# One lock in the planner's model, lower halves on VectorE, five column blocks beside the attention

## The chip, the cores and the metric

The kernel runs on one core of a Trainium2 chip. The metric is the device time of one execution in microseconds (us). A profiled execution gives a trace of every engine: TensorE (PE, its weight loads PEld), VectorE (DVE), ScalarE (ACT), GpSimd (POOL) and SyncE (SP), which here only issues transfers.

## The reference, cut to what matters

Everything is float32. Causal attention over 2 batches, 12 heads, 448 positions, head width 64; then a gated feed-forward block with RMS norm, then a second feed-forward block:

```
attn  = softmax(mask(q @ k^T / 8)) @ v            # per head, 448 x 448
x     = attn as (896 tokens, 768)
xn    = x / sqrt(mean(x*x) + 1e-6) * rms_g
h     = silu(xn @ w_gate) * (xn @ w_val)          # 768 -> 1536
y     = h @ w_out                                 # 1536 -> 768
g     = max(0.01 * (y @ w_in), y @ w_in)          # 768 -> 2048
out   = g @ w_out2                                # 2048 -> 768
```

The weights arrive as float64 (two 32-bit words each).

## The kernel before

**Products in three passes.** Every feed-forward operand is split into an upper half, rounded to the fast float type of TensorE, and a lower half, which is the rest. A product is upper x upper, upper x lower, lower x upper: lines 568, 569 and 570, one matmul of 448 columns each.

**A weight tile** (`weight`, lines 187 to 214) is loaded as 768 columns of float64 into one of two `raw` tiles, turned into float32 in one of two `x` tiles by ACT (L202) and four DVE instructions (L203, L205, L207, L209), and split into one of four `hl` tiles: upper half on ACT (L211), lower half on POOL (L212). There are 78 such tiles. A tile waits for the reader of the tile that held its place before.

**The attention** goes through 12 pairs of heads, six per batch. `maxima` (L309, L317) finds each row's largest score, which goes to DRAM and back as a row (`md`, `mrow`); `exponents` forms the scores again (L367, L373), takes exp on ACT (L396) and cuts off the masked triangle on POOL (L403). `attend` sums the exponents (L430) and multiplies by the values (L415); the sums go to DRAM and back (`sd`, `st`), are inverted on DVE (L460, L463) and spread to all partitions through DRAM (`rd`, `rb`). POOL multiplies by the inverse (L477), ACT squares (L485), and POOL adds the square to the batch's sum (L488).

**The norm** of batch b (`norm`, lines 495 to 546) follows the batch's last pair: sum over partitions (L506), DVE (L520), the power -1/2 on POOL (L522), four diagonal tiles `dg` on DVE (L525), spread by TensorE (L513), ACT (L529), then for each of six blocks of 128 channels: scale on DVE (L534), upper half on ACT (L537), lower half on POOL (L544), in the second batch on DVE for every other block (L540).

**Beside the attention of batch 1** the gate and value products of batch 0 run for the first EARLY = 6 column blocks of w_gate and w_val, in banks 4 and 5 alone, 36 matmuls a block. Each ends in `gate_out` (lines 603 to 620): silu on ACT (L611), product on DVE (L613), upper half on ACT (L616), lower half (L618) on POOL for the early blocks and on DVE for the others. The weights of the last two early blocks stay in `hl` for batch 1; those of the first EARLY - 2 are loaded and prepared a second time at the end of this stage ("again"). The other products follow when the attention is done, 2448 matmuls of lines 568 to 570 in all.

**The order of the work** is fixed in advance by the class `Order` (lines 19 to 92). Every step has an engine, an estimated cost, its dependences, a rank, a delay `late` after its end (the transfers) and an earliest time `at`. `emit` takes the engine that can start first, on it the ready step with the lowest rank, and moves a model clock; the instructions are then issued in the order of the model's starts. Each engine executes its own list in that order, so a step that is late in fact holds up what is listed behind it. All transfers are issued by SP, from one list. A lower rank goes first: pair i has ranks from 10i - 30 to 10i + 27, the norm of batch 1 has 88 and less, the early blocks 99 and up, their weights 87 and up.

Of the kernel before, what the change touches and what calls it, by code (L numbers as in the profile page):

```python
# [13 lines left out]
ALU = mybir.AluOpType  # L14
# [4 lines left out]
class Order:  # L19

    SWITCH = 0.09
    HOP = 0.12
# [5 lines left out]

    def add(self, eng, cost, fn, r=(), w=(), rank=0.0, late=0.0, mode=None, at=0.0):
        n = len(self.steps)
        deps = set()
        for k in r:
            deps.update(self.written.get(k, ()))
        for k in w:
            deps.update(self.written.get(k, ()))
            deps.update(self.read.get(k, ()))
        for k in w:  # L40
            self.written[k] = [n]
            self.read[k] = []
        for k in r:
            if k not in w:
                self.read.setdefault(k, []).append(n)
        self.steps.append((eng, cost, fn, deps, rank, late, mode, at))
        return n

    def emit(self):
        steps = self.steps  # L50
        left = [len(s[3]) for s in steps]
        users = [[] for _ in steps]
        for n, s in enumerate(steps):
            for d in s[3]:
                users[d].append(n)
        est = [s[7] for s in steps]
        ready = {}
        for n, s in enumerate(steps):
            if not left[n]:
                ready.setdefault(s[0], []).append(n)  # L60
        free = {}
        mode = {}
        start = [0.0] * len(steps)
        for _ in steps:
            best = None
            for eng, ns in ready.items():
                if ns:
                    t = max(free.get(eng, 0.0), min(est[n] for n in ns))
# [4 lines left out]
            n = min(  # L73
                (n for n in ready[eng] if est[n] <= t),
                key=lambda n: (steps[n][4] + (6 if steps[n][6] != cur else 0), n),
            )
            ready[eng].remove(n)
            _, cost, _, _, _, late, m, _ = steps[n]
            if m != cur:
                cost += self.SWITCH  # L80
                mode[eng] = m
            start[n] = t
            free[eng] = t + cost
            done = t + cost + late
            for u in users[n]:
                est[u] = max(est[u], done + (0.0 if steps[u][0] == eng and not late else self.HOP))
                left[u] -= 1
                if not left[u]:
                    ready.setdefault(steps[u][0], []).append(u)
        for n in sorted(range(len(steps)), key=lambda n: (start[n], n)):  # L90
            steps[n][2]()
        return max(free.values())
# [3 lines left out]
def causal_attention_two_ffns(  # L96
# [53 lines left out]
    def f32(ap):  # L150
        return ap.bitcast(F32)
# [5 lines left out]

    EARLY = 6
    NBIG = B * KF2
# [27 lines left out]
    def weight(key, rank, at=0.0):  # L187
# [14 lines left out]
        add("ACT", 0.85, lambda: nc.scalar.activation(x[:, :w], tf, AF.Abs), r=[kr], w=[kx], rank=rank)  # L202
        add("DVE", 0.62, lambda: nc.vector.tensor_scalar(  # L203
            x[:, :w], x[:, :w], LEAST, MOST, ALU.max, ALU.min), r=[kx], w=[kx], rank=rank)
        add("DVE", 0.6, lambda: nc.vector.tensor_scalar(  # L205
            xb, xb, 3, 0x3FFFFFF8, ALU.logical_shift_left, ALU.bitwise_and), r=[kx], w=[kx], rank=rank)
        add("DVE", 1.0, lambda: nc.vector.scalar_tensor_tensor(  # L207
            xb, top, 0xC0000000, xb, ALU.bitwise_and, ALU.bitwise_or), r=[kr, kx], w=[kx], rank=rank)
        add("DVE", 1.0, lambda: nc.vector.scalar_tensor_tensor(  # L209
            xb, low, 29, xb, ALU.logical_shift_right, ALU.bitwise_or), r=[kr, kx], w=[kx], rank=rank)  # L210
# [145 lines left out]
    def exponents(i):  # L356
# [23 lines left out]
        for kbs in groups:  # L380
# [12 lines left out]
            for j in range(2):  # L393
# [8 lines left out]
                d = d[:, :, lead:lead + P]  # L402
                add("POOL", 0.45, lambda d=d: nc.gpsimd.affine_select(  # L403
                    out=d, in_=d, compare_op=ALU.is_ge, fill=0.0, base=0, pattern=[[0, 2], [1, P]],
                    channel_multiplier=-1), w=[("p", i % 2, j, kb) for kb in kbs], rank=10 * i - 6)

    def attend(i):
# [16 lines left out]
        def sums():  # L424
            for kb in range(KB):
                for j in range(2):
# [7 lines left out]
                    )  # L434

        pk = [("p", i % 2, j, kb) for j in range(2) for kb in range(KB)]
        add("PE", 1.95 if last else 0.95, sums, r=pk, w=["sm"], rank=10 * i + 5, mode=128)
# [11 lines left out]
        else:  # L449
# [5 lines left out]
            for j in range(2):  # L455
# [3 lines left out]
            st = sts[i % NB]  # L459
            add("DVE", 0.15, lambda: nc.vector.scalar_tensor_tensor(  # L460
                out=rs[i % NB], in0=st[:, 0], scalar=1e-9, in1=st[:, 1], op0=ALU.add, op1=ALU.add),
# [12 lines left out]
        if i + 1 < NPAIR:  # L474
            add("ACT", 0.57, lambda: nc.scalar.copy(x, AV[:, :S]), r=["av"], w=[("x32", i % NX32)],
                rank=10 * i + 5)
            add("POOL", 1.1, lambda: nc.gpsimd.tensor_tensor(out=x, in0=x, in1=rbs[i % NB], op=ALU.mult),  # L477
                r=[("rb", i % NB, 0), ("rb", i % NB, 1)], w=[("x32", i % NX32)], rank=10 * i + 26)
        else:
            add("DVE", 0.65, lambda: nc.vector.tensor_tensor(  # L480
                out=x, in0=AV[:, :S], in1=rbs[i % NB], op=ALU.mult),
                r=["av", ("rb", i % NB, 0), ("rb", i % NB, 1)], w=[("x32", i % NX32)], rank=10 * i + 26)
        a = acc[:, b * S:(b + 1) * S]
        sq = sqs[i % 2] if hp else a
        add("ACT", 0.57, lambda: nc.scalar.activation(sq, x, AF.Square), r=[("x32", i % NX32)],  # L485
            w=[("sq", i % 2) if hp else ("acc", b)], rank=10 * i + 27)
        if hp:
            add("POOL", 1.1, lambda: nc.gpsimd.tensor_tensor(out=a, in0=a, in1=sq, op=ALU.add),  # L488
                r=[("sq", i % 2)], w=[("acc", b)], rank=10 * i + 27)

# [4 lines left out]
    def norm(b):  # L495
# [15 lines left out]
        def spread():  # L511
# [9 lines left out]
            r=[k0], w=[("ms", b)], rank=rank - 30)  # L521
        add("POOL", 1.4, lambda: nc.gpsimd.tensor_tensor(out=rt, in0=ms, in1=nhalf, op=ALU.pow),  # L522
            r=[("ms", b)], w=[("rt", b)], rank=rank - 30)
        for c in range(NC):
            add("DVE", 0.25, lambda c=c: nc.vector.tensor_scalar(  # L525
                dgs[c], ident[:C, :C], rt[:, c:c + 1], None, ALU.mult),
                r=[("rt", b)], w=[("dg", c)], rank=rank - 30)
        add("PE", 0.95, spread, r=[("dg", c) for c in range(NC)], w=[k1], rank=rank - 20, mode=128)
        add("ACT", 0.57, lambda: nc.scalar.copy(rsb, B1[:, :S]), r=[k1], w=["rs"], rank=rank - 20)  # L529
        for i in range(KD):  # L530
            n = (b * NP + i) % NX32
            x = x32[n]
            hi, lo = (xn[:, e, i, b * S:(b + 1) * S] for e in range(2))
            add("DVE", 0.75, lambda x=x, i=i: nc.vector.scalar_tensor_tensor(  # L534
                out=x, in0=x, scalar=gsb[:, i:i + 1], in1=rsb, op0=ALU.mult, op1=ALU.mult),
                r=["rs"], w=[("x32", n)], rank=rank + i)
            add("ACT", 0.57, lambda x=x, hi=hi: nc.scalar.copy(hi, x),  # L537
                r=[("x32", n)], w=[("xh", b, i)], rank=rank + i)
            if b and i % 2:
                add("DVE", 0.7, lambda x=x, hi=hi, lo=lo: nc.vector.tensor_tensor(  # L540
                    out=lo, in0=x, in1=f32(hi), op=ALU.subtract),
                    r=[("x32", n), ("xh", b, i)], w=[("xn", b, i)], rank=rank + i)
            else:
                add("POOL", 1.1, lambda x=x, hi=hi, lo=lo: nc.gpsimd.tensor_tensor(  # L544
                    out=lo, in0=x, in1=f32(hi), op=ALU.subtract),
                    r=[("x32", n), ("xh", b, i)], w=[("xn", b, i)], rank=rank + i)

# [55 lines left out]
    def gate_out(fc, b, rank, room, lower):  # L603
# [4 lines left out]
        def view(e):  # L608
# [8 lines left out]
            r=[("sg", s)] + room, w=[("big", n)], rank=rank)  # L617
        add(*lower, lambda: (nc.gpsimd if lower[0] == "POOL" else nc.vector).tensor_tensor(  # L618
            out=view(1), in0=sgs[s], in1=f32(view(0)), op=ALU.subtract),
# [27 lines left out]
    for n in range(NPAIR + AHEAD):  # L647
# [32 lines left out]
    for again in (False, True):  # L680
        for fc in range(EARLY - 2) if again else range(EARLY - 2, KF):
# [5 lines left out]
            for b in range(1 if kept or again else 0, B):  # L687
                for nm in "gv":
                    gate(nm, fc, b, rank, again=again)
                gate_out(fc, b, rank, ["room"], ("DVE", 0.7))  # L690

# [22 lines left out]
    for fc in range(KF2):  # L714
        rank = FF + 60 + fc
        weight(("i", fc), rank - 1)
        for b in range(B):
# [8 lines left out]
            def view(e, g=g):  # L726
# [8 lines left out]
                r=[("sg", s), "room"], w=[("big", g)], rank=rank)  # L735
            add("DVE", 0.7, lambda s=s, view=view: nc.vector.tensor_tensor(  # L736
                out=view(1), in0=sgs[s], in1=f32(view(0)), op=ALU.subtract),
# [65 lines left out]
```

## Time and profile before

| | |
|---|---|
| median of 3 runs | 648.8 us (648.07, 648.8, 654.26) |
| profiled execution | 649.93 us |
| its span, first to last instruction | 648.1 us |
| instructions | 8720 |
| TensorE busy in matmuls | 616.4 us (95%) |
| VectorE busy | 445.8 us (69%) |
| ScalarE busy | 265.3 us (41%) |
| GpSimd busy | 229.6 us (35%) |
| moved by DMA | 74.56 MB, mean 115 GB/s |

"Busy" is the share of the span in which the engine has an instruction in work. TensorE's matmuls overlap, so its busy share counts a slow or half-filled stretch as full; the granted clock and the number of matmuls in a stretch say more. An instruction of DVE or POOL that stands still because the other engine holds something also counts as busy.

### The profile page before, as it was taken

How to read it: one execution, taken by the hardware profiler on the slowest of the kernel's cores; microseconds unless marked ns; L12 is line 12 of the kernel's file. 1: busy time of each engine (PE TensorE's matmuls, PEld its weight loads, DVE VectorE, ACT ScalarE, POOL GpSimd, SP SyncE). 2: the span in 40 equal slices, each digit the busy share in tenths (PEclk: the TensorE clock that was granted, in tenths of full speed). 3: DMA queues.
4: the chain of work that ended last, by engine and by line, in shares of the span. 5: the costliest groups of instructions: out<-in, count | busy, mean ns of one | idle time of the engine just before them, and what ended most of it. 6: DMA issues, size and time to landing. Idle time of an engine off the chain costs nothing.

```text
span 648.1 us, 8720 instructions
## 1 busy us (share of the span) xinstructions
PE 616.4 (95%) x3280; PEld 531.4 (82%) x3280; DVE 445.8 (69%) x694; ACT 265.3 (41%) x406; POOL 229.6 (35%) x176
## 2 busy tenths in 40 slices
PE   8987878979889999999999999999999999999997
PEld 5654446657779999999889999999999999999996
DVE  6465579768878696558988974599999883444300
ACT  3446655664333433334433423355554543223210
POOL 1224556965542332233333322232233223132300
PEclk7799987998889999999999999999999999999999
DMA  5254642332323144322444443233223323344100
GB/s 179 76 156 130 205 135 80 114 115 90 120 97 106 67 141 141 131 98 98 146 147 147 146 147 102 93 127 116 98 99 101 123 85 119 137 139 131 62 28 30
DMA packets 21331, 74.56 MB, mean 115 GB/s; under 512 B 5220, under 2 KB 8232, under 8 KB 21288
## 3 DMA queue, kind: packets, MB, share of 16 engines
q1 hardware_dynamic: 21288, 73.99, 34.2%
q8 instruction: 26, 0.43, 0.3%
q14 instruction: 17, 0.14, 0.1%
HBM read 71.07 MB, written 2.91 MB: 114 GB/s over the span
## 4 chain that ended last, share of the span: by engine, by line
PE 76%; DVE 14%; DMA 4%; issue 3%; ACT 1%; POOL 1%; SPq 1%; DVEq 0%; ACTq 0%; POOLq 0%
PE bank L568 22%; PE bank L569 22%; PE bank L570 22%; DVE x L207 3%; PE bank L415 2%; PE bank L373 2%; DMA md<-mt 2%; DVE x L203 2%; DVE x L534 2%; DVE x L209 2%; DVE x L205 1%; PE bank L309 1%; DMA st<-sd 1%; PE bank L367 1%; DVE bank L317 1%
## 5 line engine op out<-in xcount | busy, mean ns | idle before, releaser
L212 POOL TENSOR_TENSOR hl<-x,hl 128x768 fp32r<-128x768 f32 (+1 forms) x78 | 155.1, 1990 | 315.1 <-ACT hl L211 300.6
L568 PE MATMUL bank<-xn,hl 128*128 128x448 f32 x480 | 178.8, 372 | 2.7 <-DVE sg L613 2.7
L569 PE MATMUL bank<-xn,hl 128*128 128x448 f32 x480 | 177.0, 369 | 0.0
L570 PE MATMUL bank<-xn,hl 128*128 128x448 f32 x480 | 176.9, 368 | 0.0
L569 PE MATMUL bank<-big,hl 128*128 128x448 f32 x336 | 122.9, 366 | 1.2 <-DVE big L618 1.2
L570 PE MATMUL bank<-big,hl 128*128 128x448 f32 x336 | 122.9, 366 | 0.7 <-POOL hl L212 0.7
L568 PE MATMUL bank<-big,hl 128*128 128x448 f32 x336 | 122.8, 365 | 0.0
L202 ACT ACTIVATE x<-raw 128x768 f32<-128x768 f32 (+1 forms) x78 | 69.1, 887 | 111.8 <-POOL hl L212 77.2
L203 DVE TENSOR_SCALAR x<-x 128x768 f32<-128x768 f32 (+1 forms) x78 | 51.2, 656 | 81.5 <-ACT x L202 81.5
L207 DVE SCALAR_TENSOR_TENSOR x<-raw,x 128x768 uint32<-128x768 uint32 (+1 forms) x78 | 100.4, 1287 | 2.5
L568 PEld LDWEIGHTS bank<-xn,hl 128*128 128x128 f32 x480 | 91.3, 190 | 12.7 <-ACT xn L537 3.3
L569 PEld LDWEIGHTS bank<-xn,hl 128*128 128x128 f32 x480 | 91.4, 191 | 7.3
L570 PEld LDWEIGHTS bank<-xn,hl 128*128 128x128 f32 x480 | 91.3, 190 | 7.4
L211 ACT CAST hl<-x 128x768 fp32r<-128x768 f32 (+1 forms) x78 | 63.7, 816 | 65.0 <-PE bank L569 37.8
L209 DVE SCALAR_TENSOR_TENSOR x<-raw,x 128x768 uint32<-128x768 uint32 (+1 forms) x78 | 79.6, 1021 | 1.4
L569 PEld LDWEIGHTS bank<-big,hl 128*128 128x128 f32 x336 | 63.1, 188 | 6.5 <-DVE big L618 1.5
L570 PEld LDWEIGHTS bank<-big,hl 128*128 128x128 f32 x336 | 63.1, 188 | 6.1 <-POOL hl L212 1.1
L568 PEld LDWEIGHTS bank<-big,hl 128*128 128x128 f32 x336 | 63.1, 188 | 5.0
L317 DVE CUSTOM_DVE_ANT_0 bank<-bank,maskw 112x224 f32<-112x224 f32 (+2 forms) x96 | 41.8, 464 | 25.1 <-PE bank L309 23.9
L205 DVE TENSOR_SCALAR x<-x 128x768 uint32<-128x768 uint32 (+1 forms) x78 | 49.4, 633 | 1.8
L736 DVE TENSOR_TENSOR big<-sg,big 128x448 fp32r<-128x448 f32 x32 | 45.6, 1424 | 0.0
L403 POOL TENSOR_SCALAR_AFFINE_SELECT p<-p 128x256 f32<-128x256 f32 x48 | 23.6, 503 | 48.9 <-ACT p L396 47.9
(69 smaller groups left out, 526.9 us busy)
## 6 DMA issues: line engine op xcount, KB each, us to landing
raw<-in_out SPq DMA_DIRECT2D x24, 768.0 KB
raw<-in_gate SPq DMA_DIRECT2D x16, 768.0 KB
raw<-in_val SPq DMA_DIRECT2D x16, 768.0 KB
raw<-in_in SPq DMA_DIRECT2D x16, 768.0 KB
qk<-in_qk SPq DMA_DIRECT2D x12, 448.0 KB
v<-in_v SPq DMA_DIRECT2D x12, 256.0 KB
raw<-in_out SPq DMA_DIRECT2D x6, 512.0 KB
out<-sg SPq DMA_DIRECT2D x12, 224.0 KB
```

Source lines behind the costliest of these rows:

```text
L202: add("ACT", 0.85, lambda: nc.scalar.activation(x[:, :w], tf, AF.Abs), r=[kr], w=[kx], rank=rank)
L203: add("DVE", 0.62, lambda: nc.vector.tensor_scalar(x[:, :w], x[:, :w], LEAST, MOST, ALU.max, ALU.min), r=[kx], w=[kx], rank=rank)
L205: add("DVE", 0.6, lambda: nc.vector.tensor_scalar(xb, xb, 3, 0x3FFFFFF8, ALU.logical_shift_left, ALU.bitwise_and), r=[kx], w=[kx], rank=rank)
L207: add("DVE", 1.0, lambda: nc.vector.scalar_tensor_tensor(xb, top, 0xC0000000, xb, ALU.bitwise_and, ALU.bitwise_or), r=[kr, kx], w=[kx], ra ...
L209: add("DVE", 1.0, lambda: nc.vector.scalar_tensor_tensor(xb, low, 29, xb, ALU.logical_shift_right, ALU.bitwise_or), r=[kr, kx], w=[kx], ra ...
L211: add("ACT", 0.85, lambda: nc.scalar.copy(hl[:, 0, :w], x[:, :w]), r=[kx], w=[kh], rank=rank)
L212: add("POOL", 1.95, lambda: nc.gpsimd.tensor_tensor(out=hl[:, 1, :w], in0=x[:, :w], in1=f32(hl[:, 0, :w]), op=ALU.subtract), r=[kx, kh], w ...
L317: nc.vector.tensor_tensor_reduce(out=s, in0=s, in1=maskw[:, S - w:S], scale=-1.0, scalar=3.0e38, op0=ALU.add, op1=ALU.min, accum_out=m[:, ...
L568: nc.tensor.matmul(o, hi, xh, start=s, stop=False, skip_group_check=True)
L569: nc.tensor.matmul(o, hi, xl, start=False, stop=False, skip_group_check=True)
L570: nc.tensor.matmul(o, lo, xh, start=False, stop=e, skip_group_check=True)
L736: add("DVE", 0.7, lambda s=s, view=view: nc.vector.tensor_tensor(out=view(1), in0=sgs[s], in1=f32(view(0)), op=ALU.subtract), r=[("sg", s) ...
```

## The change

The change does these things; costs in the model are in us.

- A step may be marked `port=True`. Such steps, on DVE and POOL, follow one another in the model, whichever of the two they are on.
- The lower half of a weight goes from POOL (L212) to DVE, in the norm all lower halves go to DVE, and so do those of the early blocks.
- The four diagonals of a norm go from DVE to ACT.
- EARLY is 5 instead of 6; the rank of the early blocks is 40 higher, so behind every step of the attention, and their weights may load from 30 us on instead of 40.
- The steps after the inverse (L477, L480, L485, L488) get the rank 10i + 10 instead of 10i + 26 or 27, and 10i - 20 in the last pair of each batch.

```diff
+    def add(..., port=False):
...
+        def begin(n):
+            return max(est[n], port_free) if steps[n][8] else est[n]
...
+                    t = max(free.get(eng, 0.0), min(begin(n) for n in ns))
...
+            if port:
+                port_free = t + cost
...
-    EARLY = 6
+    EARLY = 5
...
-        add("POOL", 1.95, lambda: nc.gpsimd.tensor_tensor(
+        add("DVE", 0.95, port=True, fn=lambda: nc.vector.tensor_tensor(
             out=hl[:, 1, :w], in0=x[:, :w], in1=f32(hl[:, 0, :w]), op=ALU.subtract),
...
+        own = 10 * i + (10 if (i + 1) % NP else -20)
...
-            add("DVE", 0.25, lambda c=c: nc.vector.tensor_scalar(
-                dgs[c], ident[:C, :C], rt[:, c:c + 1], None, ALU.mult),
+            add("ACT", 0.3, lambda c=c: nc.scalar.activation(
+                dgs[c], ident[:C, :C], AF.Copy, scale=rt[:, c:c + 1]),
...
-            if b and i % 2:
-                add("DVE", 0.7, lambda x=x, hi=hi, lo=lo: nc.vector.tensor_tensor(
...
-                add("POOL", 1.1, lambda x=x, hi=hi, lo=lo: nc.gpsimd.tensor_tensor(
+            add("DVE", 0.65, port=True, fn=lambda x=x, hi=hi, lo=lo: nc.vector.tensor_tensor(
...
-        return 10.0 * (NP + 3 + fc) + 9
+        return 10.0 * (NP + 7 + fc) + 9
...
-            weight((nm, fc, False), early_rank(fc) - 12, at=40.0 + 8 * (2 * fc + n))
+            weight((nm, fc, False), early_rank(fc) - 12, at=30.0 + 8 * (2 * fc + n))
...
-                    gate_out(fc, 0, early_rank(fc) - 10, [], ("POOL", 1.15))
+                    gate_out(fc, 0, early_rank(fc) - 10, [], ("DVE", 0.65, True))
```

Marked with the port are the DVE steps of a weight (L203, L205, L207, L209, L212), L403, L460, L477, L488, L522, L534, the lower halves of the norm, and L618 and L736.

## Rows read from the trace of the kernel before

**Rows 1.** The page: busy tenths of PE and granted clock in 40 slices.

```profile
PE   8987878979889999999999999999999999999997
PEclk7799987998889999999999999999999999999999
```

**Rows 2.** Windows of each stage: length, busy us (x instructions) by engine, clock, DMA.

```profile
0.00:100.00 100.00, 84.92 (x626) 52.70 (x626) 61.60 (x224) 49.72 (x81) 36.36 (x64) 0.88 0.46 144
100.00:184.40 84.40, 73.32 (x407) 55.15 (x405) 70.24 (x97) 45.30 (x70) 57.98 (x45) 0.90 0.29 98
184.40:320.00 135.60, 135.60 (x663) 125.61 (x664) 101.19 (x117) 51.85 (x77) 42.38 (x23) 0.99 0.34 117
320.00:330.00 10.00, 8.15 (x39) 6.81 (x38) 9.02 (x10) 3.99 (x6) 3.67 (x2) 1.00 0.47 159
330.00:640.00 310.00, 310.00 (x1532) 287.35 (x1531) 203.75 (x249) 113.35 (x173) 89.25 (x44) 1.00 0.33 110
```

**Rows 3.** Windows of 20 us between 100 and 200 us, same columns.

```profile
100.00:120.00 20.00, 16.59 (x110) 11.01 (x108) 19.61 (x39) 9.55 (x17) 16.28 (x15) 0.83 0.23 70
...
140.00:160.00 20.00, 16.63 (x84) 11.49 (x83) 12.79 (x19) 11.66 (x17) 11.63 (x11) 0.83 0.27 91
160.00:180.00 20.00, 18.35 (x89) 16.25 (x88) 18.17 (x22) 8.38 (x14) 12.54 (x9) 0.91 0.34 119
180.00:200.00 20.00, 17.35 (x80) 15.64 (x79) 14.72 (x18) 7.26 (x12) 8.45 (x5) 0.91 0.22 79
```

**Rows 4.** PE's waits, 100 to 185 us: for whom, us in total, times, longest.

```profile
PE bank L513 <- DVE dg L525: 3.6, 2, 2.0
PE bank L367 <- ACT p L396: 3.4, 1, 3.4
PE bank L568 <- DVE sg L613: 2.7, 1, 2.7
```

**Rows 5.** DVE by line, 100 to 184 us: busy us, mean ns | idle before.

```profile
L207 DVE SCALAR_TENSOR_TENSOR x<-raw,x 128x768 uint32<-128x768 uint32 x9 | 13.4, 1492 | 0.3
L534 DVE SCALAR_TENSOR_TENSOR x<-x,gsb,rsb 128x448 f32<-128x448 f32 x12 | 11.0, 974 | 0.2 <-ACT rsb L529 0.2
L209 DVE SCALAR_TENSOR_TENSOR x<-raw,x 128x768 uint32<-128x768 uint32 x9 | 10.6, 1175 | 0.2
L203 DVE TENSOR_SCALAR x<-x 128x768 f32<-128x768 f32 x9 | 8.8, 974 | 5.7 <-ACT x L202 5.7
L205 DVE TENSOR_SCALAR x<-x 128x768 uint32<-128x768 uint32 x9 | 7.0, 776 | 0.2
...
L525 DVE TENSOR_SCALAR dg<-ident,rt 112x112 f32<-112x112 f32 x8 | 5.7, 770 | 0.0
...
L540 DVE TENSOR_TENSOR xn<-x,xn 128x448 fp32r<-128x448 f32 x2 | 2.2, 1089 | 0.0
```

**Rows 6.** Single lines over the whole span: duration ns, min/median/max, first and last start.

```profile
L203 DVE TENSOR_SCALAR x<-x x78: 427/560/1574, 54.0 to 610.0; 128x768 f32<-128x768 f32 x72, 128x512 f32<-128x512 f32 x6
L209 DVE SCALAR_TENSOR_TENSOR x<-raw,x x78: 683/953/2485, 62.2 to 611.7; 128x768 uint32<-128x768 uint32 x72, 128x512 uint32<-128x512 uint32 x6
L534 DVE SCALAR_TENSOR_TENSOR x<-x,gsb,rsb x12: 672/680/1583, 107.8 to 182.5; 128x448 f32<-128x448 f32 x12
L525 DVE TENSOR_SCALAR dg<-ident,rt x8: 265/268/2550, 101.9 to 172.5; 112x112 f32<-112x112 f32 x8
L618 DVE TENSOR_TENSOR big<-sg,big x18: 610/616/2219, 199.3 to 328.1; 128x448 fp32r<-128x448 f32 x18
L212 POOL TENSOR_TENSOR hl<-x,hl x78: 1283/1851/2582, 75.5 to 619.5; 128x768 fp32r<-128x768 f32 x72, 128x512 fp32r<-128x512 f32 x6
```

**Rows 7.** PE's waits, 20 to 100 us, as in Rows 4.

```profile
PE bank L367 <- DMA mrow<-md: 5.9, 2, 3.4
PE bank L415 <- POOL p L403: 2.9, 2, 2.1
```

**Rows 8.** ACT lines: table load and a small copy, count, busy us, mean ns.

```profile
L611 ACT ACT_TABLE_LOAD x3 | 3.8, 1283 | 0.1
...
L529 ACT COPY rsb<-bank 128x448 f32<-128x448 f32 x2 | 1.1, 529 | 3.2 <-PE bank L513 3.2
```

More of the change, by code (lines that the diff above doesn't have):

```diff
@@ L30, in __init__, with add @@
         self.read = {}
-    def add(self, eng, cost, fn, r=(), w=(), rank=0.0, late=0.0, mode=None, at=0.0):
+    def add(self, eng, cost, fn, r=(), w=(), rank=0.0, late=0.0, mode=None, at=0.0, port=False):
         n = len(self.steps)
@@ L45, in add @@
                 self.read.setdefault(k, []).append(n)
-        self.steps.append((eng, cost, fn, deps, rank, late, mode, at))
+        self.steps.append((eng, cost, fn, deps, rank, late, mode, at, port))
         return n
@@ L61, in emit @@
         free = {}
+        port_free = 0.0
         mode = {}
         start = [0.0] * len(steps)
+        def begin(n):
+            return max(est[n], port_free) if steps[n][8] else est[n]
         for _ in steps:
@@ L67, in emit @@
                 if ns:
-                    t = max(free.get(eng, 0.0), min(est[n] for n in ns))
+                    t = max(free.get(eng, 0.0), min(begin(n) for n in ns))
                     if best is None or t < best[0]:
@@ L73, in emit @@
             n = min(
-                (n for n in ready[eng] if est[n] <= t),
+                (n for n in ready[eng] if begin(n) <= t),
                 key=lambda n: (steps[n][4] + (6 if steps[n][6] != cur else 0), n),
@@ L77, in emit @@
             ready[eng].remove(n)
-            _, cost, _, _, _, late, m, _ = steps[n]
+            _, cost, _, _, _, late, m, _, port = steps[n]
+            if port:
+                port_free = t + cost
             if m != cur:
@@ L402, in exponents @@
                 d = d[:, :, lead:lead + P]
-                add("POOL", 0.45, lambda d=d: nc.gpsimd.affine_select(
+                add("POOL", 0.45, port=True, fn=lambda d=d: nc.gpsimd.affine_select(
                     out=d, in_=d, compare_op=ALU.is_ge, fill=0.0, base=0, pattern=[[0, 2], [1, P]],
@@ L459, in attend @@
             st = sts[i % NB]
-            add("DVE", 0.15, lambda: nc.vector.scalar_tensor_tensor(
+            add("DVE", 0.15, port=True, fn=lambda: nc.vector.scalar_tensor_tensor(
                 out=rs[i % NB], in0=st[:, 0], scalar=1e-9, in1=st[:, 1], op0=ALU.add, op1=ALU.add),
@@ L476, in attend @@
                 rank=10 * i + 5)
-            add("POOL", 1.1, lambda: nc.gpsimd.tensor_tensor(out=x, in0=x, in1=rbs[i % NB], op=ALU.mult),
-                r=[("rb", i % NB, 0), ("rb", i % NB, 1)], w=[("x32", i % NX32)], rank=10 * i + 26)
+            add("POOL", 1.1, port=True, fn=lambda: nc.gpsimd.tensor_tensor(out=x, in0=x, in1=rbs[i % NB], op=ALU.mult),
+                r=[("rb", i % NB, 0), ("rb", i % NB, 1)], w=[("x32", i % NX32)], rank=own)
         else:
@@ L481, in attend @@
                 out=x, in0=AV[:, :S], in1=rbs[i % NB], op=ALU.mult),
-                r=["av", ("rb", i % NB, 0), ("rb", i % NB, 1)], w=[("x32", i % NX32)], rank=10 * i + 26)
+                r=["av", ("rb", i % NB, 0), ("rb", i % NB, 1)], w=[("x32", i % NX32)], rank=own)
         a = acc[:, b * S:(b + 1) * S]
@@ L485, in attend @@
         add("ACT", 0.57, lambda: nc.scalar.activation(sq, x, AF.Square), r=[("x32", i % NX32)],
-            w=[("sq", i % 2) if hp else ("acc", b)], rank=10 * i + 27)
+            w=[("sq", i % 2) if hp else ("acc", b)], rank=own)
         if hp:
-            add("POOL", 1.1, lambda: nc.gpsimd.tensor_tensor(out=a, in0=a, in1=sq, op=ALU.add),
-                r=[("sq", i % 2)], w=[("acc", b)], rank=10 * i + 27)
+            add("POOL", 1.1, port=True, fn=lambda: nc.gpsimd.tensor_tensor(out=a, in0=a, in1=sq, op=ALU.add),
+                r=[("sq", i % 2)], w=[("acc", b)], rank=own)
     dgs = ring(NC, [C, C], F32, "dg")
@@ L521, in norm @@
             r=[k0], w=[("ms", b)], rank=rank - 30)
-        add("POOL", 1.4, lambda: nc.gpsimd.tensor_tensor(out=rt, in0=ms, in1=nhalf, op=ALU.pow),
+        add("POOL", 1.4, port=True, fn=lambda: nc.gpsimd.tensor_tensor(out=rt, in0=ms, in1=nhalf, op=ALU.pow),
             r=[("ms", b)], w=[("rt", b)], rank=rank - 30)
         for c in range(NC):
-            add("DVE", 0.25, lambda c=c: nc.vector.tensor_scalar(
-                dgs[c], ident[:C, :C], rt[:, c:c + 1], None, ALU.mult),
+            add("ACT", 0.3, lambda c=c: nc.scalar.activation(
+                dgs[c], ident[:C, :C], AF.Copy, scale=rt[:, c:c + 1]),
                 r=[("rt", b)], w=[("dg", c)], rank=rank - 30)
@@ L533, in norm @@
             hi, lo = (xn[:, e, i, b * S:(b + 1) * S] for e in range(2))
-            add("DVE", 0.75, lambda x=x, i=i: nc.vector.scalar_tensor_tensor(
+            add("DVE", 0.75, port=True, fn=lambda x=x, i=i: nc.vector.scalar_tensor_tensor(
                 out=x, in0=x, scalar=gsb[:, i:i + 1], in1=rsb, op0=ALU.mult, op1=ALU.mult),
@@ L538, in norm @@
                 r=[("x32", n)], w=[("xh", b, i)], rank=rank + i)
-            if b and i % 2:
-                add("DVE", 0.7, lambda x=x, hi=hi, lo=lo: nc.vector.tensor_tensor(
-                    out=lo, in0=x, in1=f32(hi), op=ALU.subtract),
-                    r=[("x32", n), ("xh", b, i)], w=[("xn", b, i)], rank=rank + i)
-            else:
-                add("POOL", 1.1, lambda x=x, hi=hi, lo=lo: nc.gpsimd.tensor_tensor(
-                    out=lo, in0=x, in1=f32(hi), op=ALU.subtract),
-                    r=[("x32", n), ("xh", b, i)], w=[("xn", b, i)], rank=rank + i)
+            add("DVE", 0.65, port=True, fn=lambda x=x, hi=hi, lo=lo: nc.vector.tensor_tensor(
+                out=lo, in0=x, in1=f32(hi), op=ALU.subtract),
+                r=[("x32", n), ("xh", b, i)], w=[("xn", b, i)], rank=rank + i)
     turn = [0]
@@ L617, in gate_out @@
             r=[("sg", s)] + room, w=[("big", n)], rank=rank)
-        add(*lower, lambda: (nc.gpsimd if lower[0] == "POOL" else nc.vector).tensor_tensor(
+        add(*lower[:2], port=lower[2], fn=lambda: (nc.gpsimd if lower[0] == "POOL" else nc.vector).tensor_tensor(
             out=view(1), in0=sgs[s], in1=f32(view(0)), op=ALU.subtract),
@@ L689, in causal_attention_two_ffns @@
                     gate(nm, fc, b, rank, again=again)
-                gate_out(fc, b, rank, ["room"], ("DVE", 0.7))
+                gate_out(fc, b, rank, ["room"], ("DVE", 0.65, True))
     for dc in range(KD):
@@ L735, in causal_attention_two_ffns @@
                 r=[("sg", s), "room"], w=[("big", g)], rank=rank)
-            add("DVE", 0.7, lambda s=s, view=view: nc.vector.tensor_tensor(
+            add("DVE", 0.65, port=True, fn=lambda s=s, view=view: nc.vector.tensor_tensor(
                 out=view(1), in0=sgs[s], in1=f32(view(0)), op=ALU.subtract),
```

8 lines of the change are left out of this document (4 added, 4 removed).

## The prediction

> **What bounds the kernel now.** I read the slices first, then the windows, then what PE waits for in the windows that fall short. The slices show two regimes: PE at 7 to 9 tenths and a granted clock of 7 to 9 up to about 190 us, then both full to the end, but for one slice [rows 1]. The windows say the same in numbers [rows 2]. From 330 to 640 us PE issues 1532 instructions in 310 us without a gap, 0.202 us each, at clock 1.00; 184 to 320 us has no gap either. No work of another engine can shorten these stretches. Before 184.4 us PE lacks 15.1 us in the first 100 and 11.1 us in the next 84.4, at mean clocks of 0.88 and 0.90; 1.85 us are missing between 320 and 330. The matmuls are the same after the change, since a smaller EARLY only moves 36 of them, 7.3 us, out of the attention stage into the full stretch. So the time can change only by what PE loses before 190 us, and around 325.
>
> The stretch that the change touches is 100 to 184.4 us. PE's waits there are few and have names [rows 4]: 3.6 us on the norm's diagonals (L525), 3.4 us on an exponent (L396), 2.7 us on the product that frees a gate bank (L613), 9.7 us together. They come with clock: the windows in which they lie are granted 0.83, 0.83, 0.91 and 0.91 of full speed [rows 3], which at 20 us each is up to 0.17 + 0.17 + 0.09 + 0.09 = 0.52 windows, 10.4 us, lost beside the waits (the mean between the two levels, 1.2 and 2.4 GHz). That is 20.1 us at most.
>
> Behind the waits stands DVE, busy 70.2 of 84.4 us [rows 2], but not with work. Its lines take much longer there than their medians over the whole span [rows 5, 6]: L207 1.49 us (it has two SBUF inputs and the size of L209, 0.95), L534 0.97 against 0.68, L209 1.18 against 0.95, L203 0.97 against 0.56, L205 0.78 (like L203, 0.56), L525 0.77 against 0.27, L540 1.09 against 0.62 (L618's form). With the counts: 4.9 + 3.5 + 2.0 + 3.7 + 2.0 + 4.0 + 0.9 = 21.0 us of standing still, while POOL is busy 58.0 us, above all with L212 at 1.85 us.
>
> **The change part by part.**
>
> *Lower halves to DVE.* On DVE the trace has no L212. Below it lies L618, the same subtraction on 448 columns, 0.62 us, above it the POOL form, 1.85; I take L209, also 768 columns and two SBUF inputs: 0.95 [rows 6]. In 100 to 184 us this adds nine times 0.95 for weights, nine times 0.62 in the norms and five times 0.62 in the early blocks: 8.6 + 5.6 + 3.1 = 17.3 us. It takes away the 21.0 us of standing still as far as POOL's long steps caused it; L403, L477, L488 and L522 remain.
>
> *Diagonals to ACT.* DVE loses 8 x 0.27 = 2.1 us. On ACT no such tile is in the trace; between nothing and the 0.53 of a 448-column copy [rows 8] I take 0.3, nearer the 0.27 that it took on DVE. Four are 1.2 us on the norm's path, where two waits of 3.6 us now stand.
>
> *EARLY 5.* Two weights fewer, 2 x (0.56 + 0.56 + 0.95 + 0.95) = 6.0 us of DVE, and one L613, 0.6. The two are also not prepared a second time later. DVE in this stretch: 70.2 + 17.3 - 21.0 - 2.1 - 6.6 = 58 us, for PE work that is 7.3 us shorter. DVE is no longer what the stage waits for.
>
> *Ranks.* Early blocks and weights now stand behind every pair, and the squares of pairs 5 and 11 go first. So both norms start earlier and pair 11 no longer competes with weights. On POOL the listed order gains too: no 1.85 us step stands ahead of L403 or L488. I give this no gain of its own; it is how the 9.7 us go. What is late next: in a row that is filled by rank, a step that waits on a transfer holds what is listed behind it, L403 behind L477 on POOL, every DVE step behind L460. Such waits exist: 5.9 us in two on `mrow` and 2.9 us in two on L403 before 100 us [rows 7].
>
> *Weights from 30 us.* Four loads, of 768 KB each, reach SP's list and the DMA earlier, beside the small round trips of the pairs. It may move the 5.9 us, double them, or empty them; I take zero, with 5.9 to both sides.
>
> *Silu among exponents.* A change between L611 and L396 loads a table, 1.28 us; three are at L611 and two at L396 [rows 8]. With the gates in the gaps of the pairs there may be one change each way for five blocks, five more, 6.4 us of ACT. ACT is busy 45.3 of 84.4 us; on PE's path lies only a load before an exponent. I take none, and up to 6.4.
>
> The Trainium skill ("ScalarE: Activation LUTs", "Table sets: the hidden batching unit") advises to do all calls of one set before the other, which speaks against these ranks; it puts a switch at about 2.7 us with its drain. The trace agrees on the load, 1.283 us, and shows the exponent right behind it, so I keep 1.28; by the page five more switches would be 13.3 us (an estimate).
>
> *The full stretch.* Each of its weights costs DVE 0.95 more, hidden under PE: a block of w_in needs 3.97 + 2 x 1.24 = 6.5 us of DVE for 36 x 0.202 = 7.3 us of PE. The cover fails where weights are prepared again for one batch: 2 x 3.97 + 1.24 = 9.2 us against 7.3. Three such columns fall behind by 5.7 us, against four columns before that lost 1.85. Four `hl` tiles, two columns or 14.6 us, are the lead. I take no change; bounds: 1.85 less, and 5.7 - 1.85 = 3.9 more.
>
> **The sum.** Removed: 20.1 us at most. I give back half, 9.7: two new waits of the size of those on `mrow`, 2.95 us each [rows 7], and 1.9 us of clock with each (0.09 of a window of 20). The span goes from 648.1 to 637.7, the execution (1.83 longer) from 649.9 to 639.5. The median shown, 648.8, stands 1.1 below that execution, so 638.4; with half a us for one more table load, **639**.
>
> **Rivals.** *A: the wait changes its name.* Exponents stand behind silus and tables on ACT (6.4 us), L403 behind L477, and PE waits as often as now: of the 10.4 gained 6.4 and a window's clock, 1.9, go, and the time is 647. For it: the 3.4 us on L396, the longest wait, already was one on ACT. Against it: ACT is half idle.
>
> *B: slower; the stage keeps its end.* If pair 11 and its norm are paced by the DRAM round trips and not by DVE, xn of batch 1 is ready when it was, and the early blocks that filled the time until then are 36 matmuls short: PE stands for 7.3 us, and the time is 656. It decides at one point: the first product on batch 1's xn must start 7.3 us earlier than now to break even. For it: the waits before 100 us are on transfers [rows 7]. Against it: none of the three after 100 is [rows 4].
>
> *C: all of it goes.* No new waits: 648.8 - 20 = 629.
>
> *D: POOL was not the cause,* DVE's long instructions stay long. Then the 17.3 us come on top of 70.2 - 8.7, DVE is full for the stage, and nothing is gained: 648 to 652. Against it: the 21 us vanish in the medians, so they are not the instructions' own.
>
> **How the numbers follow.** Forecast 0.54, A 0.20, B 0.14, C 0.07, D 0.05. One per cent, about what a measurement of this kernel tells from no change, is 642.3 and 655.3 us. The forecast's own range, with 5.9 for the early loads, is 633 to 645; some 0.47 of its 0.54 is below 642.3, with C 0.54 faster. B is over 655.3 in about 0.12 of its 0.14, with a little of D 0.13 slower; 0.33 within. The range from 630 to 654 leaves out most of C and B.
>
> **What would show it.** L207, L209 and L534 at 0.96, 0.95 and 0.68 us in the attention stage; no POOL step over 1.2 us but the power; no PE wait on `dg` and under 1 us on L613; the 1033 PE instructions that stand before 184.4 us now done by about 174; the full stretch unchanged at 0.202 us. It is wrong if PE's gaps before that point are as many as now under other names (A), if batch 1's first product comes no earlier (B), or if gaps open around the weights prepared again or in the blocks of w_in.

## The result and the profile after

The changed kernel takes 623.4 us (median; 622.2 to 624.6), the kernel before 648.4 beside it: a ratio of 0.960, interval 0.955 to 0.966. That is 25 us, where 10 were forecast, and below the range. Some executions of a kernel run in a slower state: medians, ratios and intervals from here on are of the others, but the traces of `b_port`, `a_oldrank`, `a_own`, `a_at34`, `a_late` and `a_hop11` are of such slower executions.

The profiled execution has a span of 621.1 us against 648.1. The windows of its stages come first, in the columns of [rows 2]; in the lines of the changed kernel L573 to L575 are the three passes (568 to 570 before), L375 to L381 the scores, L220 the weights' lower half, L549 the norm's.

```profile
0.00:100.00 100.00, 87.53 (x670) 56.77 (x672) 69.25 (x241) 55.85 (x94) 36.55 (x64) 0.90 0.49 153
100.00:184.40 84.40, 83.28 (x476) 68.71 (x476) 72.75 (x117) 46.23 (x75) 18.72 (x19) 1.00 0.33 107
184.40:320.00 135.60, 135.60 (x671) 125.69 (x670) 101.44 (x143) 53.76 (x76) 0.00 (x0) 1.00 0.37 127
320.00:330.00 10.00, 10.00 (x51) 9.28 (x50) 8.27 (x12) 4.21 (x6) 0.00 (x0) 1.00 0.49 159
330.00:610.00 280.00, 280.00 (x1384) 259.52 (x1383) 180.72 (x260) 104.53 (x157) 0.00 (x0) 1.00 0.32 104
```

From 330 us on PE issues 1384 instructions in 280 us, 0.202 us each, as before. Everything was won ahead of that. From 100 to 184.4 us PE now stands still for 1.1 us instead of 11.1, and its clock is 1.00 throughout instead of 0.90, worth at most 0.10 x 84.4 = 8.4. In the first 100 us it stands still for 12.5 instead of 15.1, at 0.90 instead of 0.88, 2.6 + 2.0. The 1.85 us near 325 are gone, and 184 to 320 has its full clock, 1.4. Together 10.0 + 8.4 + 4.6 + 1.85 + 1.4 = 26.3 of the 27.0 us, an account in which each share of the clock is an upper bound, since a low clock costs nothing while PE stands still.

What PE waits for after 100 us, the counterpart of [rows 4], are two small items (up to 200 us; none comes later):

```profile
PE bank L574 <- DVE xn L549: 0.7, 1, 0.7
PE bank L573 <- ACT xn L547: 0.4, 1, 0.4
```

DVE's lines from 100 to 184 us, in the form of [rows 5] (L215 was L207, L544 was L534, L217 was L209, L213 was L205, L211 was L203):

```profile
L215 DVE SCALAR_TENSOR_TENSOR x<-raw,x 128x768 uint32<-128x768 uint32 x11 | 10.8, 985 | 0.1
L217 DVE SCALAR_TENSOR_TENSOR x<-raw,x 128x768 uint32<-128x768 uint32 x11 | 10.4, 946 | 0.2
L220 DVE TENSOR_TENSOR hl<-x,hl 128x768 fp32r<-128x768 f32 x10 | 9.5, 953 | 4.4 <-ACT hl L219 4.4
L549 DVE TENSOR_TENSOR xn<-x,xn 128x448 fp32r<-128x448 f32 x12 | 7.8, 684 | 0.3 <-ACT xn L547 0.2
L544 DVE SCALAR_TENSOR_TENSOR x<-x,gsb,rsb 128x448 f32<-128x448 f32 x10 | 7.3, 768 | 0.5 <-ACT rsb L539 0.5
L213 DVE TENSOR_SCALAR x<-x 128x768 uint32<-128x768 uint32 x11 | 7.1, 641 | 0.3
L211 DVE TENSOR_SCALAR x<-x 128x768 f32<-128x768 f32 x11 | 6.0, 548 | 1.5 <-ACT x L210 1.5
```

The standing still is all but gone: 0.99 us for 1.49, 0.95 for 1.18, 0.77 for 0.97, 0.64 for 0.78, 0.55 for 0.97. The weights' subtraction takes 0.95 us on DVE, the 0.95 that was estimated, against 1.85 on POOL. DVE is as busy in this stretch as before (72.8 us against 70.2; 58 were forecast), but it has eleven weights in it instead of nine.

### The profile page after: what moved, and what is told of

Same layout as the page of the kernel before. It is cut to its first block, busy times and chain, and to the rows that moved or that the text cites. A ratio compares the mean times of both kernels' runs of the same rounds, so it can differ in the third digit from the quotient of the medians.

```text
span 621.1 us, 8620 instructions
## 1 busy us (share of the span) xinstructions
PE 604.0 (97%) x3280; PEld 526.7 (85%) x3280; DVE 432.4 (70%) x769; ACT 265.6 (43%) x408; POOL 55.3 (9%) x83
## 4 chain that ended last, share of the span: by engine, by line
PE 91%; DMA 4%; DVE 3%; issue 1%; ACT 0%; SPq 0%; POOL 0%; ACTq 0%
PE bank L573 27%; PE bank L574 26%; PE bank L575 26%; PE bank L381 3%; PE bank L423 3%; PE bank L375 2%; PE bank L317 2%; PE bank L438 1%; DMA md<-mt 1%; DMA mrow<-md 1%; DVE bank L325 1%; DMA raw<-in_gate 1%; PE bank L633 1%; DMA rd<-r 1%; DVE x L544 1%
## 5 line engine op out<-in xcount | busy, mean ns | idle before, releaser
L573 PE MATMUL bank<-xn,hl 128*128 128x448 f32 x480 | 176.6, 368 | 0.4 <-ACT xn L547 0.4
L574 PE MATMUL bank<-xn,hl 128*128 128x448 f32 x480 | 175.5, 366 | 0.7 <-DVE xn L549 0.7
L575 PE MATMUL bank<-xn,hl 128*128 128x448 f32 x480 | 175.3, 365 | 0.0
L575 PE MATMUL bank<-big,hl 128*128 128x448 f32 x336 | 122.7, 365 | 0.0
L573 PE MATMUL bank<-big,hl 128*128 128x448 f32 x336 | 122.7, 365 | 0.0
L220 DVE TENSOR_TENSOR hl<-x,hl 128x768 fp32r<-128x768 f32 (+1 forms) x76 | 72.1, 948 | 60.5 <-ACT hl L219 58.6
L573 PEld LDWEIGHTS bank<-xn,hl 128*128 128x128 f32 x480 | 90.2, 188 | 9.7 <-issue 1.7
L574 PEld LDWEIGHTS bank<-xn,hl 128*128 128x128 f32 x480 | 90.2, 188 | 8.2 <-DVE xn L549 1.1
L575 PEld LDWEIGHTS bank<-xn,hl 128*128 128x128 f32 x480 | 90.2, 188 | 7.1
L219 ACT CAST hl<-x 128x768 fp32r<-128x768 f32 (+1 forms) x76 | 61.9, 815 | 72.0 <-PE bank L574 53.8
L210 ACT ACTIVATE x<-raw 128x768 f32<-128x768 f32 (+1 forms) x76 | 67.5, 888 | 57.8 <-DVE hl L220 37.6
L217 DVE SCALAR_TENSOR_TENSOR x<-raw,x 128x768 uint32<-128x768 uint32 (+1 forms) x76 | 72.2, 950 | 1.4
L215 DVE SCALAR_TENSOR_TENSOR x<-raw,x 128x768 uint32<-128x768 uint32 (+1 forms) x76 | 71.8, 945 | 1.4
L575 PEld LDWEIGHTS bank<-big,hl 128*128 128x128 f32 x336 | 63.1, 188 | 5.0
L573 PEld LDWEIGHTS bank<-big,hl 128*128 128x128 f32 x336 | 63.1, 188 | 5.0
L211 DVE TENSOR_SCALAR x<-x 128x768 f32<-128x768 f32 (+1 forms) x76 | 41.7, 549 | 33.2 <-ACT x L210 33.0
L213 DVE TENSOR_SCALAR x<-x 128x768 uint32<-128x768 uint32 (+1 forms) x76 | 42.5, 559 | 2.0
L404 ACT ACTIVATE p<-bank 128x512 f32<-128x512 f32 x48 | 26.3, 594 | 22.1 <-PE bank L381 22.0
L381 PE MATMUL bank<-qk 64*128 64x448 f32 (+3 forms) x192 | 34.1, 431 | 0.0
```

The costliest lines, as they stand in the source:

```text
L211: add("DVE", 0.62, port=True, fn=lambda: nc.vector.tensor_scalar(x[:, :w], x[:, :w], LEAST, MOST, ALU.max, ALU.min), r=[kx], w=[kx], rank= ...
L213: add("DVE", 0.6, port=True, fn=lambda: nc.vector.tensor_scalar(xb, xb, 3, 0x3FFFFFF8, ALU.logical_shift_left, ALU.bitwise_and), r=[kx], w ...
L215: add("DVE", 1.0, port=True, fn=lambda: nc.vector.scalar_tensor_tensor(xb, top, 0xC0000000, xb, ALU.bitwise_and, ALU.bitwise_or), r=[kr, k ...
L217: add("DVE", 1.0, port=True, fn=lambda: nc.vector.scalar_tensor_tensor(xb, low, 29, xb, ALU.logical_shift_right, ALU.bitwise_or), r=[kr, k ...
L220: add("DVE", 0.95, port=True, fn=lambda: nc.vector.tensor_tensor(out=hl[:, 1, :w], in0=x[:, :w], in1=f32(hl[:, 0, :w]), op=ALU.subtract), ...
L381: nc.tensor.matmul(bank[:, off:off + w], keys, t[r, 1, kb * P:], start=False, stop=True, skip_group_check=True,)
```

## The experiments

All ratios are against the kernel before, run on the same chip. Three theories stood first: **L**, POOL's long steps held DVE; **R**, the ranks put the attention first; **M**, the planner knows the lock.

**One part alone, on the kernel before.** `b_low`: the lower halves to DVE.

```diff
-        add("POOL", 1.95, lambda: nc.gpsimd.tensor_tensor(
+        add("DVE", 0.95, lambda: nc.vector.tensor_tensor(
             out=hl[:, 1, :w], ...
-            if b and i % 2:
+            if True:
...
-                    gate_out(fc, 0, early_rank(fc) - 10, [], ("POOL", 1.15))
+                    gate_out(fc, 0, early_rank(fc) - 10, [], ("DVE", 0.65))
```

Expected: 

> The kernel before, with only the lower halves (weights, norm, early blocks) moved from POOL to DVE; ranks, six early blocks, diagonals on DVE and the planner's costs without a lock stay. Theory L (POOL's long steps held DVE): DVE's long instructions shrink to their medians, and most of the 25 us come from this alone, 648 to about 630. Theory R (the ranks that put the attention first): this alone brings 5 us or less, 643 to 648, since pair 11 and its norm still stand behind weights and gates. Theory M (the planner's knowledge of the lock): 645 or more, since the order is still planned without it.

Measured: 634.1 us, 0.977 (0.968 to 0.985). Over half of the gain, some 15 us (10 to 21 by the interval), and the only part that brings much by itself. L207, L209 and L534 take 1.04, 1.10 and 0.75 us in the stage, near their medians.

`b_rank`: the ranks (`own` is 10 * i + 10, and 10 * i - 20 in pairs 5 and 11) and the load time.

```diff
-        return 10.0 * (NP + 3 + fc) + 9
+        return 10.0 * (NP + 7 + fc) + 9
-            weight(..., at=40.0 + 8 * (2 * fc + n))
+            weight(..., at=30.0 + 8 * (2 * fc + n))
-                ... rank=10 * i + 26)
+                ... rank=own)
```

Expected: 

> The kernel before, with only the ranks changed: early blocks and their weights behind every pair, weights from 30 us on, squares of pairs 5 and 11 first. Lower halves stay on POOL. Theory R: most of the 25 us, about 630, pair 11's last product (L480 before at 159.5 us) comes some 20 us earlier. Theory L: DVE still stands still behind POOL, 643 or more. Theory M: 645 or more.

Measured: 651.6 us, 1.006 (1.001 to 1.011): nothing won. The last pair did come earlier, its last inverse on DVE at 142.3 us instead of 155.6. But the fill that is left then is held up by the diagonals on DVE and by the lower halves on POOL. PE's longest waits in this kernel from 100 to 200 us:

```profile
PE bank L514 <- DVE dg L526: 3.9, 1, 3.9
PE bank L571 <- POOL hl L212: 3.5, 4, 1.2
PE bank L570 <- POOL xn L545: 2.4, 1, 2.4
PE bank L507 <- POOL acc L489: 1.7, 1, 1.7
```

`b_early5` (`EARLY = 5` alone) and `b_port` (the lock in the plan alone).

Expected: 

> The kernel before, with five early blocks instead of six and nothing else. All theories: no gain of its own, since the number of matmuls is the same; 648 if the stage ends earlier by the 7.3 us of the block, up to 656 if the stage keeps its end (the slower rival of the prediction).

Measured: 643.3 us, 0.989 (0.982 to 0.996). One block less is a small gain, not the 7.3 us of loss of the slower rival.

Expected: 

> The kernel before, with only the planner's lock between DVE and POOL (all work stays on its engine; the steps that the change marks are marked, and three lower halves on DVE cost 0.65 instead of 0.7 in the plan). Theory M: the order is now planned with the lock, most of the 25 us, about 630. Theories L and R: the lock is still there on the chip and the attention is not first, 645 to 650.

Measured: 661.1 us, 1.020 (1.013 to 1.026). Planned with the lock while the long steps stay on POOL, the kernel is slower. M alone falls.

**One part taken back, from the changed kernel.** `a_noport` takes out the two lines that move `port_free`; `a_poolall` puts L220, the norm's blocks and the early blocks' lower halves back on POOL as in the kernel before (three of the norm's stay on DVE), with their lock; `a_oldrank` restores all three rank settings; `a_early6` sets EARLY to 6.

Expected: 

> The changed kernel, planned without the lock (the marks have no effect); everything else stays. If the lock in the plan matters once the long steps have left POOL: 628 or more. If only the place of the lower halves matters: 623 as the changed kernel, since what is left on POOL (L403, L477, L488) is short.

Measured: 632.4 us, 0.973 (0.966 to 0.979), the first case.

Expected: 

> The changed kernel with the lower halves back on POOL (weights, norm blocks and early blocks as before), the lock in the plan, the ranks and five blocks kept. Theory L: the gain is gone, 645 to 660, and DVE's long instructions are back at 1.2 us and more. Theory R: 630 or less.

Measured: 645.3 us, 0.996 (0.992 to 1.001). With the lower halves on POOL again nothing of the gain is left, and DVE's L215 and L217 take 1.19 and 1.31 us in the stage, as theory L has it.

Expected: 

> The changed kernel with the old ranks (early blocks and weights among the pairs, weights from 40 us, squares at 10i + 26). Ranks alone brought nothing while the lower halves were on POOL. If they still bring nothing: 621 to 626. If they pay only once DVE is free: 630 to 636, and the last pair ends 10 us later than in the changed kernel.

Measured: 645.4 us, 0.996 (0.991 to 1.000). Worse than either theory gave, although the lower halves are on DVE.

Expected: 

> The changed kernel with six early blocks. Five alone gave 6.7 us to the kernel before. If that gain is one of its own (two weights fewer prepared twice, a block less on banks 4 and 5): about 629. If it was only room on a crowded DVE, which is now free: 621 to 626.

Measured: 626.4 us, 0.966 (0.960 to 0.972); not told apart from the changed kernel's 0.960 (0.955 to 0.966).

The ranks then one by one, and the diagonals:

```diff
# a_earlyrank
+        return 10.0 * (NP + 3 + fc) + 9
# a_own
+        own = 10 * i + 26
# a_at40
+            weight(..., at=40.0 + 8 * (2 * fc + n))
# a_dgdve: the diagonals
+            add("DVE", 0.25, port=True, fn=lambda c=c: nc.vector.tensor_scalar(
```

Expected: 

> The changed kernel with one of the three old rank settings: the early blocks and their weights 40 lower again, so among the pairs 9 to 11 and ahead of the norm of batch 1. All old ranks together gave 651. If it is the early blocks that hold up the attention: 640 to 651, and pair 11 ends about 20 us later than the 137 us of the changed kernel. If it is the squares' rank or the load time: 621 to 628.

Measured: 636.2 us, 0.982 (0.976 to 0.989). The last pair's inverse comes 19 us later than in the changed kernel, as in the first case, but the time lies between the two.

Expected: 

> The changed kernel with the squares (L477 to L488 before) at rank 10i + 26 again, in pairs 5 and 11 too. If both norms' start hangs on it: 630 to 640, with the norm's first product (L516 in the changed kernel) later than its 90.7 us. If not: 621 to 626.

Measured: 629.6 us, 0.971 (0.963 to 0.979), between the two cases; the norm's first product comes at 93.8 us.

Expected: 

> The changed kernel with the early weights loaded from 40 us on again. The prediction gave the earlier loads zero, within 5.9 us to both sides. Zero: 621 to 626. More than 629: the earlier loads are part of the gain, and the first product of the early blocks comes later.

Measured: 648.4 us, 0.998 (0.994 to 1.002). With the loads 10 us later the whole gain is gone, and the first product of the early blocks comes at 107.2 us instead of 101.2.

Expected: 

> The changed kernel with the diagonals on DVE again (marked with the lock). With POOL's long steps gone each should take its 0.27 us, not the 0.77 of the attention stage before: 621 to 625, and PE's wait for the diagonals under 1 us. If the diagonals' place matters by itself: 627 or more.

Measured: 629.7 us, 0.971 (0.966 to 0.975). PE does not wait for the diagonals at all, so their place does not explain the 6 us by itself.

Each part taken back costs 3 to 25 us; the costs add up to several times the gain. So they can't be prices that simply add. Either the parts need one another, or a fourth theory holds: **N**, that any of these edits makes the planner put out another order, and that orders differ by this much.

**A shift of the order and nothing else.** `a_hop13` sets the planner's `HOP` to 0.13 instead of 0.12 us: no instruction, engine, rank or load time changes, only the order. With it ran `a_at34` (`at=34.0 + 8 * ...`), `a_at40s4` (`at=40.0 + 4 * ...`) and `a_late` (`late=2.5` and `late=2.0` for `md` and `mrow`), then `a_hop11` and `b_hop13`, HOP of 0.11 in the changed kernel and 0.13 in the one before.

Expected: 

> The changed kernel with the planner's hop between engines at 0.13 us instead of 0.12: no work, place, rank or load time changes, only the order that comes out. Theory N (the order's fit to the real transfers decides, and the changed kernel's order is a fortunate one): 628 to 645. Theory W (the parts decide, the weights' early loads above all): 621 to 627.

Measured: 642.5 us, 0.990 (0.985 to 0.994). An order alone can take 19 of the 25 us away, as N has it.

Expected: 

> The changed kernel with the early weights from 34 us instead of 30. Theory W: between 623 and 648, near 10 us of the 25 lost, about 631 to 635. Theory N: anywhere from 625 to 648, with no relation to the 4 us.

Measured: 640.6 us, 0.986 (0.979 to 0.994), above the 631 to 635 of W.

Expected: 

> The changed kernel with the early weights from 40 us, but 4 us apart in the plan instead of 8, so that the fourth may be loaded at 52 instead of 64. Theory W (what counts is that the weights of the first blocks are ready and later ones follow closely): 621 to 630. Theory N, or a theory by which loads before 40 us are needed: 635 to 650.

Measured: 645.1 us, 0.992 (0.989 to 0.996); having the fourth tile early does not do it.

Expected: 

> The changed kernel with the two transfers of the row maxima planned at 2.5 and 2.0 us instead of 1.3 each, nearer to what they take beside weight loads. If PE's remaining waits on mrow (6.0 us in four) are the plan's optimism: the waits go, and 615 to 620. If an order that knows them only puts other work elsewhere: 622 to 640.

Measured: 633.2 us, 0.975 (0.963 to 0.986). PE's waits on `mrow` fall from 6.0 to 2.3 us, and the time is longer: the waits that are left there are not what decides.

Expected: 

> The changed kernel with the hop at 0.11 us. The eleven neighbours with lower halves on DVE lie at 626 to 651, 639 in the mean. If the changed kernel's 623 is the fortunate end of them: 630 to 648 here. If the hop of 0.13 was the exception: 621 to 627. In both, the end of the last pair (its inverse on DVE) should tell: under 143 us goes with 635 or less, over 150 with 637 or more.

Measured: 625.3 us, 0.965 (0.961 to 0.969), and its last inverse comes at 139.4 us, as the last sentence of the expectation has it. By the expectation this is the case in which the hop of 0.13 was the exception: of three orders of the same work two lie at 0.960 and 0.965 and one at 0.990, so the runs do not show that the changed kernel's order is a rare one.

Expected: 

> The kernel before with the planner's hop at 0.13 us instead of 0.12 and nothing else. If the kernel before is an ordinary one among its orders: 640 to 660. If it was a fortunate one, as the changed kernel is: 655 or more.

Measured: 644.2 us, 0.993 (0.989 to 0.997): the kernel before is an ordinary one of its kind. That makes six orders with the lower halves on POOL, at 0.989 to 1.020 and 1.001 in the mean, against 0.960 to 0.998 and 0.979 in the mean for the fourteen with lower halves on DVE listed below. Other parts differ within each group, but theory L stands on the two groups rather than on one order of each.

**What tells good orders from bad.** The same work lies in a different place. The last pair's inverse on DVE tells when the attention is done; by the rows of the timeline it starts in the changed kernel at
```profile
133.85 1.55 DVE L457 RECIPROCAL rb<-rb 128x224 f32<-128x224 f32 x1
135.69 1.55 DVE L457 RECIPROCAL rb<-rb 128x224 f32<-128x224 f32 x1
```

and in `a_hop13` at
```profile
159.21 1.55 DVE L457 RECIPROCAL rb<-rb 128x224 f32<-128x224 f32 x1
161.04 1.55 DVE L457 RECIPROCAL rb<-rb 128x224 f32<-128x224 f32 x1
```

How many of the early blocks' products (one upper by upper for every three matmuls, so 12 a block and 60 in all) PE has issued by the first of these rows is read from its lines from 0 to 133.85 us in the changed kernel,

```profile
L573 PE MATMUL bank<-xn,hl 128*128 128x448 f32 x27 | 10.7, 397 | 0.0
```

and from 0 to 159.21 us in `a_hop13`:

```profile
L573 PE MATMUL bank<-xn,hl 128*128 128x448 f32 x54 | 20.7, 383 | 1.1 <-ACT xn L547 1.1
```

In the changed kernel 33 of 60 are still to come then, 33 x 3 x 0.202 = 20 us of matmuls, and they cover the norm of batch 1: the 60th product starts at 155.54 us, and the next, on batch 1's xn, right behind it. In `a_hop13` only 6 are left, 3.6 us, and the last pair ends 25 us later; the 60th starts at 172.61 us, and the next waits until 179.52. The rows of the changed kernel, then those of `a_hop13`:

```profile
155.54 0.37 PE L573 MATMUL bank<-xn,hl 128*128 128x448 f32 x1
156.15 0.37 PE L573 MATMUL bank<-xn,hl 128*128 128x448 f32 x1
...
172.61 0.57 PE L573 MATMUL bank<-xn,hl 128*128 128x448 f32 x1
179.52 0.74 PE L573 MATMUL bank<-xn,hl 128*128 128x448 f32 x1 [1.94 <-ACT xn L547]
```

The windows of `a_hop13` around that (columns of [rows 2]) show the cost:

```profile
140.00:160.00 20.00, 19.94 (x109) 15.86 (x107) 16.96 (x23) 8.50 (x13) 5.52 (x7) 1.00 0.39 134
160.00:184.40 24.40, 14.40 (x43) 11.86 (x44) 16.45 (x24) 7.21 (x15) 2.81 (x2) 0.60 0.20 65
```

From 160 us on PE stands still for 10.0 of 24.4 us, at a clock of 0.60, where the changed kernel has none and 1.00. Beside the 1.94 us above, its waits there are on weights and on the norm's diagonals, with the start of the matmul, its busy time, and in brackets the wait:

```profile
166.07 0.74 PE L575 MATMUL bank<-xn,hl 128*128 128x448 f32 x1 [6.13 <-DVE hl L220]
175.53 2.05 PE L523 MATMUL bank<-dg,ones 112*128 112x112 f32 x8 [1.60 <-ACT dg L535]
```

The 6.13 us are also a matter of order: on DVE the subtraction that PE needs is listed behind the last pair's two inverses (159.2 to 162.6 us), and is done at 166.0.

The same for all kernels with lower halves on DVE (72 early products instead of 60 in `a_early6` and `b_low`, which have six blocks). The fourth column has the start of the first of the last pair's two inverses:

| kernel | median us | ratio | last inverse from, us | products before it |
|---|---|---|---|---|
| changed | 623.4 | 0.960 | 133.9 | 27 |
| a_hop11 | 625.3 | 0.965 | 137.6 | 27 |
| a_early6 | 626.4 | 0.966 | 138.3 | 27 |
| a_dgdve | 629.7 | 0.971 | 141.2 | 38 |
| a_own | 629.6 | 0.971 | 137.4 | 28 |
| a_noport | 632.4 | 0.973 | 136.7 | 23 |
| a_late | 633.2 | 0.975 | 149.0 | 49 |
| b_low | 634.1 | 0.977 | 148.7 | 34 |
| a_earlyrank | 636.2 | 0.982 | 153.0 | 60 |
| a_at34 | 640.6 | 0.986 | 155.4 | 54 |
| a_hop13 | 642.5 | 0.990 | 159.2 | 54 |
| a_at40s4 | 645.1 | 0.992 | 156.1 | 51 |
| a_oldrank | 645.4 | 0.996 | 147.4 | 34 |
| a_at40 | 648.4 | 0.998 | 153.6 | 44 |

The five with 28 products or fewer lie at 0.973 or below; of the nine with more, only `a_dgdve` does. The start of the last inverse parts the first six rows from the other eight without exception: before 142 us the ratio is 0.973 or less, after 147 us 0.975 or more, though the border itself is not clear of noise. And in the lower eight but `b_low`, PE waits 1.9 to 2.7 us for the first of batch 1's upper halves (L547), in the others at most 0.4 for any of them: where PE waits, the fill had run out. It isn't the whole of it: `a_oldrank` has waits of 13.4 us on `mrow` besides, all before 108 us. With the lower halves on POOL an early end and a small count are no help (`a_poolall` 137.6 us and 18, `b_rank` 140.5 and 17, at 0.996 and 1.006). An early end of the attention and much fill left go together here, so these runs do not tell which of the two pays. This is a relation over the runs; a kernel that holds the early blocks back by force and is else the same was not run, so the cause is narrowed by it and not shown by itself.

## Why the prediction was wrong, point by point

*What bounds it, and the full stretch:* right. The time moved only by what PE lost before 190 us and around 325; 0.202 us an instruction held.

*Lower halves, lock:* right in mechanism and size. L220 takes 0.95 us, DVE's long instructions went to their medians or near (0.99, 0.95 and 0.77 us where 0.96, 0.95 and 0.68 were named as signs), POOL has 18.7 us in the stage instead of 58.0, though L487 still takes 1.36 us where no step over 1.2 was to be left. `a_poolall` and the two groups of orders show that the gain hangs on it, `b_low` that it is worth some 15 us without the other parts. *Diagonals:* PE's wait on them is gone, but it is gone in `a_dgdve` too, with the diagonals on DVE.

*The step that failed* is "I give back half, 9.7: two new waits of the size of those on `mrow`". After 100 us there are no such waits; PE lost 1.1 us, and the clock came back entirely. 10.0 + 8.4 us went in the stage and 1.4 of clock behind it, 19.8 of the 20.1, so the 9.7 was too much by 9.4. This was rival C, held at 0.07, and the terms that were taken as zero went the same way: 4.6 before 100 us and 1.85 near 325, which carried the time below C's 629. These three make 15.9 of the 16.6 us by which the span, 621.1, lies below the forecast 637.7. The 1033rd PE instruction was done at 162 us, where 174 was forecast. What gained the 4.6 us before 100 was not separated.

*Behind it stands the step on ranks,* "I give this no gain of its own". Not the ranks alone: `b_rank` gains nothing, and `a_hop13` has the changed kernel's ranks and 642.5. But the order that comes out of ranks, costs, lock and load times moved the time by up to 19 us (`a_hop13`), and with it whether the attention ends early and the early blocks last until the norm of batch 1 is done. Where it doesn't, that is rival B's mechanism: batch 1's first upper half starts at 177.8 us in the kernel before (L537), at 154.6 in the changed one (L547), and at 178.9 in `a_hop13`. So in `a_hop13` the stage does keep its end, with the fill spent. B was priced as one block, 7.3 us, and as a matter of round trips; it is a matter of where the plan puts the blocks. The prediction priced the parts as if the order were fixed. An estimate of the parts without the order: the mean ratio of the twelve `a_` kernels of the table is 0.980, about 13 us, though most of them have one part taken back; the other 12 would then be this order's, and that much of the result is luck, since nothing in the forecast chose this order. With only the three orders of the unchanged parts, 0.960, 0.965 and 0.990, the split is not known better than that.

*Weights from 30 us,* zero within 5.9: `a_at40` loses 25, but `a_hop13` loses 19 with the early loads kept. The runs do not show a price of the load time by itself.

*EARLY 5:* 3 us or less in the changed kernel, not clear of noise, and 7 in the one before, each time with another order. *Silu among exponents:* three table loads among L616 and L404 instead of five among L611 and L396, so none was added.

*Rival A* (an ACT wait in place of the others) did not come: no wait of PE on an exponent after 100 us. *Rival D* is excluded by DVE's durations.

## What to carry to other kernels

Where a static order is planned from modelled times, an edit has two effects, the part's own and that of the new order; shift a number in the planner that changes no work, two or three times, before a gain or a loss is given to a part. Filler work that is meant to cover a late stage is worth most if it is still there when that stage begins: count how much of it is left at that point. Taking long instructions off a resource that two engines share gave some 15 us here by itself, in the one order that was run, and ranks that put the critical work first gave nothing while those instructions stayed; the 25 us came with both, in an order that fits.

## What the runs showed of the hardware that was not expected

In the 24.4 us in which `a_hop13` lets PE stand still for 10.0, the granted clock is 0.60, a mean between the two levels of 1.2 and 2.4 GHz. After the pause of 6.13 us matmuls of 448 columns start 0.37 us apart instead of 0.21, and they do so until about 185 us. So the stretch costs clock beside the waiting: an estimate is 6 us, from the 27 such matmuls in it at 0.17 us each and 1.7 us for L516 and L523 (1.51 and 2.05 us instead of 0.85 and 1.04 in the changed kernel).
